# First block of a Fourier-mixing kernel: G's products in other accumulator banks, another order of a step, and identity products in TensorE's waits

## The chip, the cores and the metric

The kernel runs on one core of one Trainium2 chip. The metric is the time of the whole kernel on the device, in microseconds; the profile is one execution taken by the hardware profiler, and all positions in it are counted from the start of its span.

## What is computed

```python
X = np.fft.fft(x, axis=1)            # x: (8, 3008, 256)
X = np.fft.fft(X, axis=2)
h = X.real.reshape(8 * 3008, 256) @ w_in     # w_in: (256, 2048)
r = np.maximum(h, 0.0)
out = (r * r) @ w_out                # w_out: (2048, 256)
```

Everything is float32. The real part of the two transforms is a sum of a cosine part and a sine part. The transform along the rows (3008 long) is made by products with cosine and sine tables, after folding rows that share a table value. The transform along the 256 columns is not made on the data at all: it is multiplied into w_in, which gives a matrix G. G1 holds the cosine rows, G2 the sine rows, and gE the row of the alternating column (+1, -1, ...).

## The kernel before, in words

**The opening.** VectorE folds the rows of batch 0, tile by tile: `for_p(t)` makes the cosine half of tile t and `for_q(t)` its sine half (lines 356 to 386). TensorE multiplies the folded tiles by the tables. There are six transforms (cosine, alternating column, sine, each for two parities), each of five pieces: `even_n` (products of four tiles, L455, and a copy of the first part by ScalarE, L463), `join_4` and `join_2` (sums and differences on VectorE, L468 to L472), `odd_n` (products of three tiles of 377 columns, L455) and `join_1` (the last sums into Pt, Qt or Et, L468 to L472). Piece i of the list is `groups[i]`; `i % 5` is 0 for `even_n` and 3 for `odd_n`. The order in which pieces and folds are issued is written out by hand in the calls of `groups_at`, `for_p` and `for_q`. The tables cosT and sinT are loaded on the same DMA queue behind x.

**Weights.** w_in and w_out come as 8-byte floats, and each of 16 pieces (`load_win(j)`, `load_wout(j)`) is made float32 on the chip. Such a conversion has a beginning (two VectorE instructions, L234 and L239, and three ScalarE ones, L236, L237 and L241) and a `finish` (three VectorE instructions, L244 to L247). A piece of w_in is then multiplied by the cosine and sine tables of the columns (cosd, sind; L262), and ScalarE copies the results from PSUM into G1 and G2 (L263); four more products with the column altd give gE (L268), which ScalarE scales by 0.5 (L270). The conversions run one ahead of their use (`next_weight`).

**The blocks.** A batch is cut into blocks of up to 251 columns (CK), and a block has eight steps, j = 0 to 7 (NJ). In a step `front` makes two pairs of products with G1 and G2 (hP L551, hQ L552) in the two buffers of tag h, and VectorE makes g from each pair (L554, L556, L557). `combine` applies Relu and Square on ScalarE (L566, L567). `back` multiplies g by w_out two steps later (LAG). In the very first block, i < 8, w_out's sums are not there yet, so `back` is plain: eight products into the accumulators mA and mB (L591). From the second block on it takes seven products with sums of g (GpSimd, L574 to L577) and of w_out, into mA to mD (L604). The first block's steps also carry the conversions: after `back`, the products for the next G are issued (the list `products`), in the same PSUM buffers of tag h that `front` uses, and then the conversions of one piece (first step, last two steps) or two. Side work for the next batch is issued by `between` from the second block on.

PSUM has 2 buffers of tag h, 2 of tag d (the transforms, pe), and the four accumulators mA to mD. In the first block mC and mD are allocated but nothing is written into them.

Of the kernel before, what the change touches and what calls it, by code (L numbers as in the profile page):

```python
# [8 lines left out]
F32 = mybir.dt.float32  # L9
# [4 lines left out]
P = 128  # L14
# [67 lines left out]
def kernel(  # L82
# [12 lines left out]
    nc = tc.nc  # L95
# [65 lines left out]
    sind = const.tile([P, 2, P - 1], F32, name="sind")  # L161
    altd = const.tile([P, 2, 1], F32, name="altd")
# [6 lines left out]
    G2 = const.tile([P - 1, F], F32, name="G2")  # L169
    gE = const.tile([P, NFC], F32, name="gE")  # L170

    def load_table(tab, src, engine):
# [16 lines left out]
    for dst, src in ((cosd, cos_d), (sind, sin_d), (altd, alt_d)):  # L189
        nc.scalar.dma_start(out=dst, in_=src.rearrange("(c p) m -> p c m", p=P))  # L190


    def pair_in(j):
# [59 lines left out]
    def load_win(j):  # L253

        w = ep.tile([P, 2, CH], F32, name="win", tag="sB" if j % 2 else "sA")
        finish = convert(parts(w, 1), pair_in(j))

        def products():
            for tab, G, n in ((cosd, G1, P), (sind, G2, P - 1)):
                ps = psh.tile([P, CH], F32, name="pg", tag="h")  # L260
                for i in range(2):
                    nc.tensor.matmul(ps[0:n], tab[:, i], w[:, i], start=i == 0, stop=i == 1)  # L262
                nc.scalar.copy(G.rearrange("p (h j f) -> j p h f", h=2, j=NJ)[j],  # L263
                               ps[0:n].rearrange("p (h f) -> p h f", h=2))
            ps = psd.tile([P, CH], F32, name="pe", tag="d")
            for h in range(2):
                for i in range(2):
                    nc.tensor.matmul(ps[:, h:h + 1], w[:, i, h * P:(h + 1) * P], altd[:, i],  # L268
                                     start=i == 0, stop=i == 1)
            nc.scalar.mul(gE[:, j::NJ], ps[:, 0:2], 0.5)  # L270

        return finish, products

    def load_wout(j):

        return convert(wout[:, j].rearrange("p h c e -> p h (c e)"), pair_out(j)), lambda: None

    def sum_wout(j):

# [261 lines left out]
    def front(b, k0, n, j, between):  # L541

        pt, qt, et = PQE[b]
        ks = slice(k0, k0 + n)
        g = gp.tile([P, 2, 2, CK], F32, name="g", tag="g")
        for h in range(2):
            fc = j + NJ * h
            fs = slice(fc * P, (fc + 1) * P)
            ps = psh.tile([P, 2, CH], F32, name="ph", tag="h")
            hP, hQ = ps[:, 0, 0:n], ps[:, 1, 0:n]  # L550
            nc.tensor.matmul(hP, G1[:, fs], pt[:, ks], start=True, stop=True)  # L551
            nc.tensor.matmul(hQ, G2[:, fs], qt[:, ks], start=True, stop=True)  # L552
# [29 lines left out]
    def back(n, j, g, s, final):  # L582

        if j == 0:
            for nm in ("mA", "mB", "mC", "mD"):
# [15 lines left out]
        if final and j == NJ - 1:  # L601
            products = products[0:2] + products[4:7] + products[2:4]
        for nm, i, w, v in products:
            nc.tensor.matmul(acc[nm][:, i, 0:n], w, v[:, 0:n], start=j == 0 and i == 0, stop=j == NJ - 1,  # L604
                             skip_group_check=True)

    def gather(n, plain, final):


        mA, mB, mC, mD = (acc[nm] for nm in ("mA", "mB", "mC", "mD"))  # L610
        if plain:
            c = ep.tile([P, 2, 2, CK], F32, name="c", tag="c")
            for side, m in enumerate((mA, mB)):
                nc.scalar.copy(c[:, side, :, 0:n], m[:, :, 0:n])
            return c
        sA = ep.tile([P, 2, CK], F32, name="sA", tag="sA")
# [12 lines left out]
        gt(out=c[:, 0, 0, 0:n], in0=m1, in1=m2, op=ALU.add)  # L629
        if final:  # L630
            tt(out=c[:, 0, 1, 0:n], in0=u4, in1=mB[:, 1, 0:n], op=ALU.add)
            tt(out=c[:, 1, 1, 0:n], in0=u3, in1=mB[:, 1, 0:n], op=ALU.add)
            tt(out=c[:, 1, 0, 0:n], in0=u3, in1=mB[:, 0, 0:n], op=ALU.subtract)
            return c
        gt(out=c[:, 1, 0, 0:n], in0=u3, in1=m4, op=ALU.subtract)
        gt(out=c[:, 1, 1, 0:n], in0=u3, in1=m5, op=ALU.add)
        gt(out=c[:, 0, 1, 0:n], in0=u4, in1=m5, op=ALU.add)
        return c
# [41 lines left out]
                + groups + [(0.0, lambda: load_e(1))])  # L680


    weights = [lambda j=j: load_win(j) for j in range(2)]
    for j in range(NJ):
        weights.append(lambda j=j: load_wout(j))
        if j + 2 < NJ:
            weights.append(lambda j=j: load_win(j + 2))

    def next_weight():

        nonlocal begun
        (finish, products), begun = begun, weights.pop(0)() if weights else None
        finish()
        return products

    pieces = [fold(0, t) for t in range(NT)]
    start, *groups = [f for _, f in dft_ops(0)]

# [8 lines left out]
    def groups_at(*which):  # L707
        for i in which:
            groups[i]()

    begun = weights.pop(0)()
# [13 lines left out]
    for_q(0)  # L725
    for_q(1)
    groups_at(1, 2)
    for_p(5)
    groups_at(6, 7)
    for_p(6)  # L730
# [4 lines left out]
    groups_at(9, 10)  # L735
    for_q(6)
    groups_at(11, 12, 13)
    begun = weights.pop(0)()
    groups_at(15)
    for_q(2)  # L740
    groups_at(14, 16, 17, 18)
    for_q(3)
    groups_at(20, 19, 25)
    products = [next_weight()]
    groups_at(21, 22, 23, 26, 27, 28)
    next_weight()
    groups_at(24, 29)
    LAG = 2
    BLOCKS = [(k0, min(CK, NKT - k0)) for k0 in range(0, NKT, CK)]
    steps = [(b, k0, n, j) for b in range(B) for k0, n in BLOCKS for j in range(NJ)]  # L750
# [3 lines left out]
    def between():  # L754
# [109 lines left out]
```

## Time and profile before

| | |
|---|---|
| time, median of 3 | 1964.85 us (1961.53 to 1965.37) |
| span of the profile | 1964.0 us |
| TensorE busy | 1929.5 us, 98% |
| VectorE busy | 1399.8 us, 71% |
| ScalarE busy | 924.9 us, 47% |
| GpSimd busy | 1170.2 us, 60% |
| first front of the first block (L554) starts | 56.75 us |
| products of step 7 of the first block (L551) start | 110.22 us |

"Busy" is an average over stages with different limits: the table alone does not tell what a change in the first 110 us is worth. For this the page's slices, windows of a few microseconds and the timelines of the engines are needed. In a timeline row the first number is the start, the second the duration, and square brackets give the idle time before it and what ended it. PEclk is the clock that TensorE was granted, as a share of full speed. One float32 product shows as two records of TensorE (x2), each with a weight load (PEld).

### The profile page before, as it was taken

Reading aid. Unit: us, or ns where it says so; the run is one execution under the profiler, and the core shown is the slowest. Engines: PE = TensorE matmul, PEld = TensorE weight load, DVE = VectorE, ACT = ScalarE, POOL = GpSimd, SP = SyncE. Lnnn points to the kernel's source line nnn. Section 1 sums busy time; section 2 is a strip of 40 time slices with the busy share of each in tenths; the row PEclk is TensorE's granted clock in tenths of the full one; section 3 lists DMA queues with packets and bytes.
Section 4 is the critical chain, followed back from the end, with each engine's and each line's share of the span. In section 5 each row is a group of like instructions: output and inputs, shape, how many; then the busy total and the mean of one; then the engine's idle time right before and its main releaser. Section 6 shows DMA issues by size and latency. Waiting matters only on the chain.

```text
span 1964.0 us, 27513 instructions
## 1 busy us (share of the span) xinstructions
PE 1929.5 (98%) x9160; PEld 1708.3 (87%) x9160; DVE 1399.8 (71%) x3434; ACT 924.9 (47%) x1076; POOL 1170.2 (60%) x1705
## 2 busy tenths in 40 slices
PE   5999999999999999999999999999999999999998
PEld 4788888888988889888988889888898888988887
DVE  7889866777677776777667776677767777656554
ACT  1654544445344544444444454444544454444443
POOL 0026745667566765666557765666756676556564
PEclk7999999999999999999999999999999999999999
DMA  6332101210121111111011200121002101100101
GB/s 186 113 50 52 27 13 39 50 27 20 16 51 41 21 29 27 40 30 38 11 35 33 48 19 11 35 54 27 19 15 53 33 11 22 27 11 11 22 11 22
DMA packets 145340, 68.88 MB, mean 35 GB/s; under 512 B 129003, under 2 KB 136110, under 8 KB 145197
## 3 DMA queue, kind: packets, MB, share of 16 engines
q1 hardware_dynamic: 144121, 66.60, 15.4%
q8 instruction: 72, 1.18, 0.2%
q10 hardware_dynamic: 1076, 0.52, 0.1%
q14 instruction: 71, 0.58, 0.1%
HBM read 42.39 MB, written 24.68 MB: 34 GB/s over the span
## 4 chain that ended last, share of the span: by engine, by line
PE 93%; DVE 3%; DMA 1%; ACT 1%; issue 0%; SPq 0%; DVEq 0%; ACTq 0%
PE ph L552 16%; PE ph L551 16%; PE mC L604 16%; PE mA L604 16%; PE mB L604 16%; PE mD L604 8%; PE pd L455 3%; PE pd L500 2%; DMA xt<-in_x_dram 1%; DVE he L554 1%; DMA raw<-in_moe_w_in_dram 1%; DVE g L557 0%; DVE g L556 0%; ACT g L566 0%; ACT g L567 0%; DMA cosT<-in_cos_s_dram 0%
## 5 line engine op out<-in xcount | busy, mean ns | idle before, releaser
L566 ACT ACTIVATE g<-g 128x1004 f32<-128x1004 f32 (+1 forms) x384 | 399.5, 1040 | 818.7 <-DVE g L557 421.3
L574 POOL TENSOR_TENSOR s<-g 128x251 f32<-128x251 f32 (+1 forms) x376 | 246.1, 655 | 718.9 <-ACT g L567 657.5
L554 DVE SCALAR_TENSOR_TENSOR he<-Et,gE,ph 128x251 f32<-128x251 f32 (+1 forms) x768 | 361.8, 471 | 421.5 <-PE ph L552 420.4
L551 PE MATMUL ph<-Pt,G 128*128 128x251 f32 (+1 forms) x1536 | 451.8, 375 | 4.2 <-ACT G L263 3.4
L552 PE MATMUL ph<-Qt,G 127*128 127x251 f32 (+1 forms) x1536 | 451.4, 374 | 0.2 <-DVE Qt L468 0.2
L567 ACT ACTIVATE g<-g 128x1004 f32<-128x1004 f32 (+1 forms) x384 | 399.2, 1040 | 12.2
L604 PE MATMUL mC<-s,wsum 128*128 128x251 f32 (+1 forms) x1504 | 381.4, 374 | 0.0
L604 PE MATMUL mA<-g,wout 128*128 128x251 f32 (+1 forms) x1504 | 379.8, 374 | 0.0
L556 DVE TENSOR_TENSOR g<-he,ph 128x251 f32<-128x251 f32 (+1 forms) x768 | 320.5, 417 | 54.4 <-POOL s L574 0.5
L551 PEld LDWEIGHTS ph<-Pt,G 128*128 128x128 f32 x1536 | 287.2, 189 | 42.2 <-ACT G L263 4.0
L552 PEld LDWEIGHTS ph<-Qt,G 127*128 127x128 f32 x1536 | 291.2, 190 | 36.4 <-DVE Qt L468 0.6
L604 PEld LDWEIGHTS mC<-s,wsum 128*128 128x128 f32 x1504 | 285.5, 190 | 34.6
L557 DVE TENSOR_TENSOR g<-he,ph 128x251 f32<-128x251 f32 (+1 forms) x768 | 314.2, 409 | 0.0
L604 PEld LDWEIGHTS mA<-g,wout 128*128 128x128 f32 x1504 | 282.8, 189 | 34.7 <-issue 0.6
L575 POOL TENSOR_TENSOR s<-s,g 128x251 f32<-128x251 f32 (+1 forms) x376 | 283.3, 754 | 29.5
L576 POOL TENSOR_TENSOR s<-g 128x251 f32<-128x251 f32 (+1 forms) x376 | 295.3, 785 | 0.0
L577 POOL TENSOR_TENSOR s<-g,s 128x251 f32<-128x251 f32 (+1 forms) x376 | 255.1, 678 | 0.0
L604 PE MATMUL mB<-g,wsum 128*128 128x251 f32 (+1 forms) x752 | 220.5, 374 | 0.0
L604 PE MATMUL mD<-s,wout 128*128 128x251 f32 (+1 forms) x752 | 220.3, 374 | 0.0
L604 PE MATMUL mB<-s,wout 128*128 128x251 f32 (+1 forms) x752 | 219.9, 374 | 0.0
L604 PEld LDWEIGHTS mB<-g,wsum 128*128 128x128 f32 x752 | 142.6, 190 | 17.4
L604 PEld LDWEIGHTS mD<-s,wout 128*128 128x128 f32 x752 | 141.9, 189 | 17.7
(118 smaller groups left out, 1292.1 us busy)
## 6 DMA issues: line engine op xcount, KB each, us to landing
out_dram<-os SPq DMA_DIRECT2D x376, 56.0 KB
xt<-in_x_dram SPq DMA_DIRECT2D x32, 384.0 KB
xt<-in_x_dram SPq DMA_DIRECT2D x42, 128.0 KB
Et<-e_dram SPq DMA_DIRECT2D x7, 752.5 KB
xt<-in_x_dram SPq DMA_DIRECT2D x9, 512.0 KB
out_dram<-os SPq DMA_DIRECT2D x288, 6.8 KB
raw<-in_moe_w_in_dram SPq DMA_DIRECT2D x16, 256.0 KB
raw<-in_moe_w_out_dram SPq DMA_DIRECT2D x16, 256.0 KB
```

Of the source, the lines that this page charges most:

```text
L551: nc.tensor.matmul(hP, G1[:, fs], pt[:, ks], start=True, stop=True)
L552: nc.tensor.matmul(hQ, G2[:, fs], qt[:, ks], start=True, stop=True)
L554: nc.vector.scalar_tensor_tensor(out=t, in0=et[:, ks], scalar=gE[:, fc:fc + 1], in1=hP, op0=ALU.mult, op1=ALU.add)
L556: tt(out=g[:, h, 0, 0:n], in0=t, in1=hQ, op=ALU.add)
L557: tt(out=g[:, h, 1, 0:n][:, ::-1], in0=t, in1=hQ, op=ALU.subtract)
L566: act(v, v, AF.Relu)
L567: act(v, v, AF.Square)
L574: gt(out=s1, in0=g21, in1=g22, op=ALU.add)
L575: gt(out=s2, in0=s1, in1=g11, op=ALU.subtract)
L576: gt(out=s3, in0=g11, in1=g21, op=ALU.subtract)
L577: gt(out=s4, in0=g12, in1=s2, op=ALU.subtract)
L604: nc.tensor.matmul(acc[nm][:, i, 0:n], w, v[:, 0:n], start=j == 0 and i == 0, stop=j == NJ - 1, skip_group_check=True)
```

## The change

It does five things.

1. Identity products: `awake(n)` issues n products of the identity matrix with itself, 128 x 128, into a buffer in mB that nothing reads. 36 stand ahead of all other TensorE work, 12 behind the first products of G, and five behind each `even_n` and each `odd_n` of the opening. They are for keeping TensorE's clock up while it waits.
2. The products for G go to the accumulators mC and mD, which the first block does not use, rather than to the buffers of tag h.
3. gE comes from G2: the alternating column is the 128th column of sind, so G2 has it as row 127, and two products with the last column of the identity bring it to a column. VectorE scales it by 0.5 in place of ScalarE.
4. A step of the first block is issued in another order: behind `front` the beginning of a conversion of w_out, the products of the next G, the finish of w_in's conversion and the beginning of the one after; then Relu and Square, then `back`, then gE's products, the finish of w_out's conversion and gE's scaling. Conversions of w_in run two steps ahead.
5. In the opening, only the conversion of piece 1 of w_in is finished and that of piece 2 begun; the conversion of piece 0 of w_out, which was finished there, moves into step 1.

```diff
+    filled = psm.tile([P, CH], F32, name="filled", tag="mB")
+    def awake(n):
+        for _ in range(n):
+            nc.tensor.matmul(filled[:, 0:P], ident, ident, start=True, stop=True)
...
         def products():
-            for tab, G, n in ((cosd, G1, P), (sind, G2, P - 1)):
-                ps = psh.tile([P, CH], F32, name="pg", tag="h")
+            for tab, G, nm in ((cosd, G1, "mC"), (sind, G2, "mD")):
+                pg = psm.tile([P, CH], F32, name="pg", tag=nm)
...
+        def for_e():
             ps = psd.tile([P, CH], F32, name="pe", tag="d")
             for h in range(2):
-                for i in range(2):
-                    nc.tensor.matmul(ps[:, h:h + 1], w[:, i, h * P:(h + 1) * P], altd[:, i],
-                                     start=i == 0, stop=i == 1)
-            nc.scalar.mul(gE[:, j::NJ], ps[:, 0:2], 0.5)
+                fc = j + NJ * h
+                nc.tensor.matmul(ps[:, h:h + 1], G2[:, fc * P:(fc + 1) * P], ident[:, P - 1:], start=True, stop=True)
+            return lambda: nc.vector.tensor_scalar_mul(gE[:, j::NJ], ps[:, 0:2], 0.5)
...
     def groups_at(*which):
         for i in which:
             groups[i]()
+            if i % 5 in (0, 3):
+                awake(5)
...
     start()
+    awake(36)
     for_p(0)
-    finish, products = begun
+    finish, products, for_e = win[0]
     finish()
     products()
+    awake(12)
     for t in range(1, 4):
         for_p(t)
     groups_at(0, 5)
...
     groups_at(1, 2)
+    for_e()()
     for_p(5)
...
-    products = [next_weight()]
-    groups_at(21, 22, 23, 26, 27, 28)
-    next_weight()
-    groups_at(24, 29)
+    win.append(load_win(2))
+    win[1][0]()
+    groups_at(21, 22, 23, 26, 27, 28, 24, 29)
...
+    def weights():
+        now = i - 1 if i < NJ - 1 else i
+        late = [load_wout(now)] if now >= 0 else []
+        if i + 1 < NJ:
+            win[i + 1][1]()
+        if i + 2 < NJ:
+            win[i + 2][0]()
+        if i + 3 < NJ:
+            win.append(load_win(i + 3))
+        elif i == NJ - 2:
+            late.append(load_wout(i))
+        def rest():
+            if i + 1 < NJ:
+                late.append(win[i + 1][2]())
+            for f in late:
+                f()
+        return rest
...
             g = front(b, k0, n, j, between)
             if i < NJ:
+                rest = weights()
                 s = combine(n, g, True)
...
-        for f in products:
-            f()
-        products = [next_weight() for _ in range(2 if 0 < i < NJ - 2 else 1 if i < NJ else 0)]
+        if i < NJ:
+            rest()
```

More of the change, by code (lines that the diff above doesn't have):

```diff
@@ L160 @@
     cosd = const.tile([P, 2, P], F32, name="cosd")
-    sind = const.tile([P, 2, P - 1], F32, name="sind")
-    altd = const.tile([P, 2, 1], F32, name="altd")
+    sind = const.tile([P, 2, P], F32, name="sind")
     cosT = const.tile([P, 2, WT], F32, name="cosT")
@@ L168 @@
     G1 = const.tile([P, F], F32, name="G1")
-    G2 = const.tile([P - 1, F], F32, name="G2")
+    G2 = const.tile([P, F], F32, name="G2")
     gE = const.tile([P, NFC], F32, name="gE")
@@ L188 @@
     nc.vector.memset(ramp[:, 1:2], 255.0 * 2.0 ** 23)
-    for dst, src in ((cosd, cos_d), (sind, sin_d), (altd, alt_d)):
+    for dst, src in ((cosd, cos_d), (sind[:, :, 0:P - 1], sin_d), (sind[:, :, P - 1:], alt_d)):
         nc.scalar.dma_start(out=dst, in_=src.rearrange("(c p) m -> p c m", p=P))
+    filled = psm.tile([P, CH], F32, name="filled", tag="mB")
+    def awake(n):
+        for _ in range(n):
+            nc.tensor.matmul(filled[:, 0:P], ident, ident, start=True, stop=True)
     def pair_in(j):
@@ L258, in products @@
         def products():
-            for tab, G, n in ((cosd, G1, P), (sind, G2, P - 1)):
-                ps = psh.tile([P, CH], F32, name="pg", tag="h")
+            for tab, G, nm in ((cosd, G1, "mC"), (sind, G2, "mD")):
+                pg = psm.tile([P, CH], F32, name="pg", tag=nm)
                 for i in range(2):
-                    nc.tensor.matmul(ps[0:n], tab[:, i], w[:, i], start=i == 0, stop=i == 1)
+                    nc.tensor.matmul(pg, tab[:, i], w[:, i], start=i == 0, stop=i == 1)
                 nc.scalar.copy(G.rearrange("p (h j f) -> j p h f", h=2, j=NJ)[j],
-                               ps[0:n].rearrange("p (h f) -> p h f", h=2))
+                               pg.rearrange("p (h f) -> p h f", h=2))
+        def for_e():
             ps = psd.tile([P, CH], F32, name="pe", tag="d")
             for h in range(2):
-                for i in range(2):
-                    nc.tensor.matmul(ps[:, h:h + 1], w[:, i, h * P:(h + 1) * P], altd[:, i],
-                                     start=i == 0, stop=i == 1)
-            nc.scalar.mul(gE[:, j::NJ], ps[:, 0:2], 0.5)
-        return finish, products
+                fc = j + NJ * h
+                nc.tensor.matmul(ps[:, h:h + 1], G2[:, fc * P:(fc + 1) * P], ident[:, P - 1:], start=True, stop=True)
+            return lambda: nc.vector.tensor_scalar_mul(gE[:, j::NJ], ps[:, 0:2], 0.5)
+        return finish, products, for_e
     def load_wout(j):
-        return convert(wout[:, j].rearrange("p h c e -> p h (c e)"), pair_out(j)), lambda: None
+        return convert(wout[:, j].rearrange("p h c e -> p h (c e)"), pair_out(j))
     def sum_wout(j):
@@ L551, in front @@
             nc.tensor.matmul(hP, G1[:, fs], pt[:, ks], start=True, stop=True)
-            nc.tensor.matmul(hQ, G2[:, fs], qt[:, ks], start=True, stop=True)
+            nc.tensor.matmul(hQ, G2[0:P - 1, fs], qt[:, ks], start=True, stop=True)
             t = hp.tile([P, CK], F32, name="he", tag="he")[:, 0:n]
@@ L584, in back @@
         if j == 0:
-            for nm in ("mA", "mB", "mC", "mD"):
+            for nm in ("mA", "mB") if s is None else ("mA", "mB", "mC", "mD"):
                 acc[nm] = psm.tile([P, 2, CH], F32, name=nm, tag=nm)
@@ L607, in gather @@
     def gather(n, plain, final):
-        mA, mB, mC, mD = (acc[nm] for nm in ("mA", "mB", "mC", "mD"))
+        mA, mB = acc["mA"], acc["mB"]
         if plain:
@@ L615, in gather @@
             return c
+        mC, mD = acc["mC"], acc["mD"]
         sA = ep.tile([P, 2, CK], F32, name="sA", tag="sA")
@@ L680, in ahead @@
                 + groups + [(0.0, lambda: load_e(1))])
[L683 to L694, printed above, removed]
     pieces = [fold(0, t) for t in range(NT)]
@@ L709, in groups_at @@
             groups[i]()
-    begun = weights.pop(0)()
+            if i % 5 in (0, 3):
+                awake(5)
+    win = [load_win(0)]
     for t in range(NT):
@@ L737 @@
     groups_at(11, 12, 13)
-    begun = weights.pop(0)()
+    win.append(load_win(1))
     groups_at(15)
```

## The prediction

> **What bounds the kernel now.** I read the page first, then windows of the opening 60 us, then the timeline of each engine there, then the chain of waits through one step of the first block.
>
> The page: TensorE is busy for 98% of the span, and one slice, the first (49 us), stands out.
>
> ```profile
> PE   5999999999999999999999999999999999999998
> DVE  7889866777677776777667776677767777656554
> PEclk7999999999999999999999999999999999999999
> ```
>
> So anything the change can win or lose lies ahead of about 115 us. After it TensorE is the bound (windows of 10 us from 120 to 200 show 9.48 to 10.00 busy), and a shift of its start is carried to the end one for one. Two stretches are separate: the opening (to 55 us) and the first block's eight steps (55 to 115 us).
>
> The windows of the opening, each 3.4 us. Columns: length, PE, PEld, DVE, ACT, POOL busy, PEclk, DMA share, GB/s.
>
> ```profile
> 16.00:19.40 3.40, 0.62 (x7) 0.57 (x6) 3.26 (x9) 0.33 (x2) 0.00 (x0) 0.97 0.57 124
> ...
> 22.80:26.20 3.40, 3.16 (x9) 2.03 (x8) 3.17 (x12) 0.30 (x2) 0.00 (x0) 0.50 1.00 251
> 26.20:29.60 3.40, 2.61 (x4) 1.46 (x5) 3.26 (x10) 0.00 (x0) 0.00 (x0) 0.50 0.33 71
> 29.60:33.00 3.40, 3.40 (x7) 1.92 (x6) 2.63 (x7) 0.00 (x0) 0.00 (x0) 0.52 0.83 241
> 33.00:36.40 3.40, 3.39 (x15) 2.03 (x14) 2.96 (x9) 0.24 (x1) 0.00 (x0) 1.00 1.05 279
> 36.40:39.80 3.40, 1.49 (x9) 1.06 (x8) 2.73 (x9) 1.81 (x3) 0.00 (x0) 0.98 1.06 369
> ```
>
> Half clock from 19.4 to 33, full clock only after a window in which TensorE was busy throughout, half again after a window with 1.49 of 3.40 busy. VectorE is busy 2.6 to 3.3 of 3.4 us throughout: it is nearly the bound here too, and its gaps, from the timeline of VectorE, are only 1.40 (22.9), 0.87 (33.3), 0.60 (a DMA), 1.68 (45.0), 0.40 and 0.89 (55.4) us. Removing every one of them gives 6 us: no more than that can be won in the opening.
>
> A step of the first block, from the chain of waits (start, us, engine, tile and line):
>
> ```profile
> 73.80 1.05 ACT g L566
> ...
> 75.91 0.53 ACT G L263 x2
> ...
> 76.52 0.62 ACT fd L236
> ...
> 77.16 0.73 ACT fd L237
> ...
> 77.92 0.69 DVE fd L244
> ```
>
> The same stretch in the timelines of TensorE and VectorE, with the idle time before a row in brackets:
>
> ```profile
> 74.78 0.95 PE L268 MATMUL pe<-altd,win 128*128 128x1 f32 x8
> 76.22 0.69 PE L551 MATMUL ph<-Pt,G 128*128 128x251 f32 x2 [0.49 <-ACT G L263]
> 77.92 0.69 DVE L244 SCALAR_TENSOR_TENSOR fd<-raw,fd 128x512 uint32<-128x512 uint32 x1 [0.75 <-ACT fd L237]
> ```
>
> A step takes 8.50 us (VectorE's front starts at 71.36, 79.85, 88.35), and the chain is a loop: front, Relu and Square on ScalarE, the copies of G and the conversion's activations queued behind them, VectorE's conversion, the next front. VectorE waits 0.75 us in it, TensorE about 0.8.
>
> [...] records of 377 columns start 0.63 us apart at half clock and 0.31 at full, and the clock flips at multiples of 3.4 us. [...] the eight one-column records above take 0.95 us with some 0.17 of tail, 0.11 each[...].
>
> **The change part by part.**
>
> 1. *Price of an identity product.* It is two records of 128 columns. Warm, 251 columns take 0.21 us (products of L551 start 0.43 apart for two records), so 128 take 0.107; the load floor is 0.11. Some pairs may not overlap fully: 0.22 to 0.27 for a product, I take 0.24, so five cost 1.2. Cold: 2 x 0.213 = 0.43, five 2.1.
>
> 2. *36 + 12 ahead of the transform.* 36 run from about 1.4 us, 8 to 16 of them cold: 8 x 0.43 + 28 x 0.24 = 10.2 to 16 x 0.43 + 20 x 0.24 = 11.7, ending at 11.6 to 13.1. They lie in the 11.96 us before win's first product; a delay of up to 1 us there is hidden, as G is next read by the new gE product at about 27. The 12 end near 17. After that the cosine tables are still landing (loads of group 0 are at 19.36, 20.07, 21.59), TensorE does only some 1 us of work in 17.5 to 21.5, and by the 36.40 row the clock then drops. So I expect group 0 and 5 cold as before: the 48 gain nothing.
>
> 3. *gE's new place.* The product is queued behind group 0, five, group 5, five; its scaling (a 128x2 row, 0.1 us) is now on VectorE behind the joins of group 0 and **ahead of for_p(5)**. Behind it wait everything VectorE does, and TensorE's group 3. Group 0 ends at 22.5; 2.1 cold; group 5 cold 2.0 (22.6 to 24.7 now), 26.6; five partly warm 1.2, 27.8; hence gE at about 28.1. VectorE reaches it at 23.9 (its last join starts at 23.62): a new wait of 4.2 us (2.0 if warm: 22.1 + 1.1 + 1.0 + 1.1 + 0.6 = 25.9). Then for_p(5), the joins and for_p(6) end at 32.2 where they ended at 28.05.
>
> 4. *The fives in the opening.* From there TensorE has group 3's last product 0.63, groups 8, 13, 18, 23, 28 at 1.89 each (6 x 0.314) and 10, 15, 20, 25 at about 1.0 each: 14.1 us warm. Between them stand nine fives, 45 x 0.24 = 10.8. 32.2 + 24.9 = 57.1, if it never waits and never goes cold. It will do both about once, after its wait for VectorE at 28 to 31: a window at half clock costs 1.7 us, partly in the wait's shadow, so I add 1.5: group 28 ends at 58.6; now it ends at 55.4. Warm products save about 10 us of TensorE here, and the products that keep it warm cost 10.8: that is the whole account. The conversion of wout 0 (2.6 us of VectorE) leaves the opening, but VectorE is no longer what ends it. **Opening: +3.2 us.**
>
> 5. *The steps.* pg goes to mC and mD instead of the pair that the front reads: no wait for L557. pe: two products for four, -0.5 us. G's copies move ahead of Relu and Square: no 0.49 wait. Then TensorE needs 1.7 + 1.7 + 3.4 + 0.5 = 7.3 and VectorE 2.33 (front) + 2 x 0.67 + 2.0 + 1.95 + 0.1 = 7.75, which becomes the bound. Step 0 has one conversion: 5.0. Step 1 goes by ScalarE's order: from front 0, win 3's activations start at 4.6 and take 2.1, Relu and Square 2.1, wout 0's 2.1, G's copies 0.6; then pe 0.7, hP and hQ 0.9, hops 0.3: front 2 at 13.4, so step 1 takes 8.4. TensorE idles some 4 us in it, so that step 2 starts cold: +1.0. Steps 2 to 4: 7.75. Step 5: 7.3. From front 6 to step 7's products: 2.7 + 2.1 + 0.6 + 0.9 = 6.3. Sum 5.0 + 8.4 + 1.0 + 23.25 + 7.3 + 6.3 = 51.3; now 56.75 to 110.22 = 53.5. **Steps: -2.2 us.** This holds though one conversion more (wout 0) is in them.
>
> 6. *Nothing:* the third table into sind's last column (same three DMAs), G2's row 127, mC and mD unallocated in the first block, one activation less a step (ScalarE had room).
>
> Sum +1.0; VectorE reaches step 8 about 2 us further behind TensorE than now, for which I add 0.1. 1964.85 + 1.1 = 1966.0.
>
> **Rivals.** *The clock comes and goes (slower).* If the fives don't fill whole windows where VectorE makes TensorE wait, two windows of 30 to 37 us are cold (1.7 each) and step 2 loses 0.9 more; with 0.27 for a product (45 x 0.03 = 1.35) the opening is 57.1 - 55.4 + 3.4 + 1.35 = +6.5, the steps -1.3: +5.2, 1970.0. For: the 22.80 row stayed cold with 3.16 of 3.40 busy. Against: the fives fill just those gaps. *The clock holds (faster).* Warm from 19.4 on at 0.22 a product: gE's wait is 2.0, so TensorE's tail starts at 30.1 and takes 14.1 + 9.9 = 24.0, to 54.1: opening -1.3; steps without the cold spell -3.2; sum -4.5: 1960.4. [...] Against: the sparse work up to 21.5. *VectorE swallows it (no change):* from 130 to 160 VectorE is 9.46 to 9.52 of 10 us busy, so if it sets the pace there once it lags, TensorE's lead after the steps (-2.2) is lost and only the opening's +3.2 shows: 1968.1.
>
> **How the numbers follow.** The likeliest case, with the last rival near it, has 0.5 and spreads over -2.5 to +3.5; the slow rival 0.28, the fast one 0.22. The range 1961.0 to 1971.0 leaves out half of the fast case and the end of the slow one, 2 in 10 together. A change under 3.9 us (0.2%) counts as none: faster 0.22, same 0.5, slower 0.28.
>
> **What would show it.** Right: the scaling of gE waits 2 to 4.5 us for TensorE at 24 to 28; from 32 us TensorE has hardly an idle gap; the first front starts at about 60; steps 2 to 4 are 7.7 to 7.9 apart; the clock drops in step 1. Wrong: full clock at 22 to 27; identity products over 0.27 or under 0.22 us; steps still 8.5 apart, or under 7.5; VectorE waiting for raw loads; a changed rate after 120 us.

## The result, and the profile after

The changed kernel takes 1968.9 us (median; 1968.51 to 1970.36). The kernel before, run beside it on the same chip, takes 1963.82 us (1959.88 to 1965.37). The ratio, taken over the runs and not from the two medians, is 1.003, 95% interval 1.0018 to 1.0043: slower by about 0.3%. The forecast was 1966.0, range 1961 to 1971. The time lies in the range, but the change was forecast as 1.1 us and is 5.1 us between the medians, and the likeliest outcome of the forecast was "no change".

The two profiled executions differ less than the medians: spans of 1964.0 and 1966.7 us. The one of before was among the slower of its kernel (1965.78 us), the one of after the fastest of its kernel (1968.51 us). Both differences have to be explained.

The page of after. The first slice is fuller for TensorE and less full for VectorE, and its clock is up:

```profile
PE   8899999999999999999999999999999999999998
...
DVE  6899866777677776777667776677767777655554
...
PEclk9999999999999999999999999999999999999999
```

That is what identity products do to an average: 49 us at nearly full clock, and a later end. What follows is where the time lies.

**The opening.** Windows of after, in before's columns (length, PE, PEld, DVE, ACT, POOL busy, PEclk, DMA share, GB/s):

```profile
17.00:20.40 3.40, 0.89 (x4) 0.79 (x4) 3.23 (x10) 0.00 (x0) 0.00 (x0) 0.91 0.37 74
20.40:23.80 3.40, 3.15 (x13) 2.62 (x13) 1.60 (x7) 0.24 (x1) 0.00 (x0) 0.50 0.84 250
23.80:27.20 3.40, 3.40 (x18) 3.40 (x18) 0.26 (x2) 0.24 (x1) 0.00 (x0) 0.58 0.85 181
34.00:37.40 3.40, 3.40 (x22) 2.64 (x21) 3.33 (x10) 0.00 (x0) 0.00 (x0) 1.00 0.54 174
```

The column PEclk, read in short windows, has half clock from 19.8 to 26.6. In before it has it from 19.2 to 32.9, and in truth TensorE was slow there from its start: the four records of win's first product at 11.96 took 2.08 us, where they take 1.02 in a later step (81.43). In after they take 1.10 (11.77): of the records of the 36 identity products ahead of them, 20 lie in the 4.23 us up to 5.60 and 49 in the 5.27 us from 6.50, which is 0.42 and 0.22 us a product. So the clock comes up while they run, and it is at half again from 19.8, when TensorE has just begun the transform (19.36) after 2.95 us without work. From 26.6 the clock is full to 71.0, through the windows where before's had dropped twice more (39.7 to 46.5 and 49.9 to 53.3). But VectorE does 0.26 us of work in 23.80 to 27.20, where it had been nearly always busy. The timelines of TensorE and VectorE in after say why (start, us, engine, line and tile; in brackets the idle time before the row and its releaser):

```profile
22.48 2.34 PE L197 MATMUL filled<-ident 128*128 128x128 f32 x10
...
26.68 1.28 PE L197 MATMUL filled<-ident 128*128 128x128 f32 x10
27.79 0.50 PE L278 MATMUL pe<-ident,G 128*128 128x1 f32 x4
28.33 0.16 DVE L280 TENSOR_SCALAR gE<-pe 128x2 f32<-128x2 f32 x1 [4.28 <-PE pe L278]
...
32.51 0.90 PE L465 MATMUL pd<-cosT,w 120*128 120x377 f32 x2 [1.67 <-DVE w L396]
...
57.15 1.28 PE L197 MATMUL filled<-ident 128*128 128x128 f32 x10
59.32 0.48 DVE L564 SCALAR_TENSOR_TENSOR he<-Et,gE,ph 128x251 f32<-128x251 f32 x1 [0.96 <-PE ph L562]
```

Five identity products at half clock (2.1 us) and five at full clock (1.1 us) stand in TensorE's queue ahead of gE's two products. VectorE stands at gE's scaling for 4.28 us, with all its folds behind it. From 32.51 TensorE no longer waits, and the first front starts at 59.32 instead of 56.75: 2.57 us later.

**The steps.** By TensorE the order of a step does what it should: from the first front to step 7's products are 51.53 us, where they were 53.47. But the first front to the fifteenth takes 90.34 us (59.32 to 149.66), where it took 90.11 (56.75 to 146.86). So nothing is won. Two places stand out. The first, step 1, is contained in the 51.53 us and keeps the gain small. Timelines of ScalarE and TensorE of after:

```profile
67.98 0.71 ACT L243 ACTIVATE fd<-fd,ramp 128x512 f32<-128x512 uint32 x1
68.72 0.72 ACT L244 ACTIVATE fd<-fd,ramp 128x512 uint32<-128x512 f32 x1
69.35 0.66 ACT L248 ACTIVATE raw<-raw 128x512 f32<-128x512 uint32 x1
69.90 0.63 ACT L270 COPY G<-pg 128x256 f32<-128x256 f32 x2
...
70.58 0.66 PE L278 MATMUL pe<-ident,G 128*128 128x1 f32 x4 [4.12 <-ACT G L270]
```

The products of G were done at about 66.4 (the last begin at 65.65), but the copies stand on ScalarE behind Relu and Square and behind the three activations of w_out's conversion. TensorE waits 4.12 us, and its clock is at half from 71.0 to 74.4. The forecast had both, with "some 4 us".

The second place, the end of the stretch, takes back what was won. VectorE and TensorE of after, steps 6 and later:

```profile
109.12 0.69 DVE L251 SCALAR_TENSOR_TENSOR fd<-raw,fd 128x512 uint32<-128x512 uint32 x1 [0.54 <-ACT fd L244]
...
110.85 0.67 PE L561 MATMUL ph<-Pt,G 128*128 128x251 f32 x2
...
111.59 0.69 DVE L251 SCALAR_TENSOR_TENSOR fd<-raw,fd 128x512 uint32<-128x512 uint32 x1 [0.45 <-ACT fd L244]
...
113.80 0.47 DVE L564 SCALAR_TENSOR_TENSOR he<-Et,gE,ph 128x251 f32<-128x251 f32 x1
...
118.09 0.69 DVE L251 SCALAR_TENSOR_TENSOR fd<-raw,fd 128x512 uint32<-128x512 uint32 x1 [1.21 <-ACT fd L244]
...
123.10 0.69 PE L561 MATMUL ph<-Pt,G 128*128 128x251 f32 x2 [0.64 <-DVE g L567]
...
143.40 0.69 PE L561 MATMUL ph<-Pt,G 128*128 128x251 f32 x2 [0.89 <-DVE g L567]
```

The fronts of the same stretch in VectorE's timeline of before:

```profile
111.44 0.48 DVE L554 SCALAR_TENSOR_TENSOR he<-Et,gE,ph 128x251 f32<-128x251 f32 x1 [1.08 <-PE ph L552]
...
116.47 0.48 DVE L554 SCALAR_TENSOR_TENSOR he<-Et,gE,ph 128x251 f32<-128x251 f32 x1 [0.69 <-PE ph L552]
...
121.58 0.47 DVE L554 SCALAR_TENSOR_TENSOR he<-Et,gE,ph 128x251 f32<-128x251 f32 x1 [0.31 <-PE ph L552]
...
126.69 0.48 DVE L554 SCALAR_TENSOR_TENSOR he<-Et,gE,ph 128x251 f32<-128x251 f32 x1 [1.15 <-PE ph L552]
```

In before VectorE came first and waited for TensorE: its slack (the time it has to spare) was 1.08, 0.69, 0.31 and 1.15 us at fronts 7 to 10, 3.23 in all. At front 11 (132.12) there is no wait: from there VectorE has no slack in before either. In after, step 6 holds two conversions of w_out and step 7 one, each with a wait for ScalarE (0.54, 0.45 and 1.21 us), and step 6 takes 8.98 us. Front 7 starts 2.36 us later than in before (113.80 against 111.44), though TensorE made its products only 0.63 us later (110.85 against 110.22). Now VectorE has no wait at fronts 7 to 11, and TensorE waits for the front's buffers. How much later after is than before, step by step:

| position | later than before, us |
|---|---|
| first front | 2.57 |
| products of step 7 (TensorE) | 0.63 |
| products of step 9 | 0.80 |
| products of step 10 | 1.81 |
| front 11 to front 14 | 2.8 |
| end of the span | 2.7 |

From front 6, which was 0.53 us earlier than in before, to front 11, VectorE had 6.6 us more to do or to wait for than in before (30.10 us, against 26.77 with 3.23 of waits in them); 3.23 of that fell into the slack. From front 11 on the fronts keep their distance, and from 143.4 on TensorE has it too.

### The profile page after: what moved, and what is told of

It reads as the page before. It is cut to its first block, busy times and chain, and to the rows that moved or that the text cites. A ratio compares the mean times of both kernels' runs of the same rounds, so it can differ in the third digit from the quotient of the medians.

```text
span 1966.7 us, 27897 instructions
## 1 busy us (share of the span) xinstructions
PE 1943.3 (99%) x9344; PEld 1727.8 (88%) x9344; DVE 1402.9 (71%) x3442; ACT 924.5 (47%) x1068; POOL 1169.1 (59%) x1705
## 4 chain that ended last, share of the span: by engine, by line
PE 93%; DVE 4%; DMA 1%; ACT 1%; issue 0%; SPq 0%; DVEq 0%; ACTq 0%
PE ph L561 16%; PE ph L562 16%; PE mC L614 16%; PE mA L614 16%; PE mB L614 16%; PE mD L614 8%; PE pd L465 3%; PE pd L510 2%; PE filled L197 1%; DVE he L564 1%; DMA xt<-in_x_dram 1%; DVE g L566 1%; DVE g L567 1%; DVE m L253 0%; DVE fd L251 0%
```

## The experiments

Times are medians, each compared with the kernel before run in the same sitting (its medians: 1963.7 to 1964.1). The opening is counted from the first copy of group 0 (tile da, by ScalarE) to the first front, because that copy starts anywhere between 21.1 and 23.3 us from one execution to the next; the transform's products ahead of it wait for the tables (2.77 us for cosT in before, 2.95 in after). The steps are the first front to the fifteenth. The last two columns come from one profiled execution each.

| kernel | time, us | ratio to before (95%) | opening | steps |
|---|---|---|---|---|
| before, trace above | | | 34.12 | 90.11 |
| before_again (one run) | 1963.41 | | 31.78 | 90.10 |
| after | 1968.9 | 1.003 (1.0018 to 1.0043) | 36.59 | 90.34 |
| no_identity | 1965.78 | 1.0007 (0.9998 to 1.0016) | 32.50 | 90.85 |
| no_fives | 1966.19 | 1.0009 (1.0001 to 1.0018) | 32.74 | 90.91 |
| ge_late | 1966.89 | 1.0012 (1.0003 to 1.0021) | 34.46 | 91.50 |
| identity_alone | 1965.13 | 1.0002 (0.9993 to 1.001) | 33.83 | 90.09 |
| wout0_opening | 1968.67 | 1.0027 (1.0016 to 1.0038) | 36.82 | 90.44 |
| steps_alone | 1966.86 | 1.0012 (1.0005 to 1.0019) | 34.79 | 91.06 |
| steps_wout0 | 1964.94 | 1.0008 (0.9999 to 1.0017) | 34.15 | 89.44 |
| g_first | 1967.28 | 1.0019 (1.0011 to 1.0027) | 37.29 | 88.73 |
| banks_alone | 1964.1 | 1.0 (0.9992 to 1.0009) | 31.32 | 90.26 |
| steps_wout0_g_first | 1961.92 | 0.999 (0.9981 to 0.9999) | 34.15 | 87.04 |

### The kernel before once more: how much the opening moves by itself

The same code, to see whether the changes of the clock fall elsewhere.

> The kernel before, unchanged, for a second trace of its opening. Theory (its spread of several us comes from where the clock's windows fall and when the tables land): another set of half-clock stretches, with the first front moved by 0.5 us or more against the first trace and the steps from the first front on within 0.3 us of it. Rival (the spread comes from elsewhere): the same opening, and a difference after 60 us.

The windows of this execution:

```profile
22.80:26.20 3.40, 3.40 (x11) 2.71 (x10) 3.10 (x11) 0.36 (x2) 0.00 (x0) 0.50 0.97 272
26.20:29.60 3.40, 2.27 (x7) 1.05 (x6) 3.26 (x10) 0.00 (x0) 0.00 (x0) 0.97 0.41 91
```

In the execution of the prediction the same window was 3.16 of 3.40 busy and the clock stayed at half until 32.9. Here it was 3.40, and the clock rose at its end, at 26.4. The first front starts at 54.47 instead of 56.75 while the steps differ by 0.01 us, and the spans differ by 2.4 us. VectorE waits for TensorE's products for 4.3 us in the opening of the one and for 1.5 in that of the other, so the difference comes in at TensorE, at half clock to 32.9 in the one and to 26.4 in the other; that the place of the clock's changes alone made it, two executions can't show. So the profile that I forecast from had an opening on the slow side, and one and the same code moves by 2.3 us there. The openings without identity products in the table lie between 31.3 and 34.8, but part of that is their code.

### Identity products: all away, the fives away, or alone

```diff
# no_identity, from after
-        for _ in range(n):
+        for _ in range(0):
# no_fives, from after (the 36 and the 12 stay)
-            if i % 5 in (0, 3):
-                awake(5)
# identity_alone, from before: filled and awake as in after, and
+            if i % 5 in (0, 3):
+                awake(5)
...
     start()
+    awake(36)
...
     products()
+    awake(12)
```

> The changed kernel without any identity product (all 36, 12 and 60 left out; nothing of the output depends on them). Theory (the fives delay gE's scaling, which VectorE waits for, and then fill TensorE; their price eats the clock's gain): gE's scaling waits only about 1.6 us instead of 4.3, the opening is at half clock again, the first front starts at about 58 (59.3 with them), the steps are unchanged, so 1 us faster than the changed kernel, about 1968. Rival (the identity products earn their place, the loss is elsewhere): the opening at half clock costs 3 us or more beyond the changed kernel's, first front at 62 or later, 1972.

> The changed kernel with the 36 and the 12, without the fives. Theory (the 48 gain nothing, since TensorE is cold again before the tables have landed): within 0.7 us of the kernel without any identity product, about 1968. Rival (the 48 keep the clock up for groups 0 and 5): full clock from 19 to 26 us, gE's wait under 1 us, 2 us faster than without any, 1966.

> The kernel before with the identity products alone (36, 12 and five behind each even_n and odd_n; gE and the steps as before). Theory (without gE's wait the clock's gain of about 10 us of TensorE and the products' 10.8 nearly cancel, and the opening is a little shorter): first front at 54.5 to 56.5, the whole 0.5 to 2.5 us faster than the kernel before. Rival (the products stand in the way): 2 us or more slower than the kernel before.

Without any of them the changed kernel takes 1965.78 us, about 3 us less where 1 was expected, and its interval (to 1.0016) lies below that of after (from 1.0018). Its first front, expected at about 58, starts at 54.42. The wait for gE, in VectorE's timeline of no_identity:

```profile
24.68 0.16 DVE L280 TENSOR_SCALAR gE<-pe 128x2 f32<-128x2 f32 x1 [1.42 <-PE pe L278]
```

1.42 us instead of 4.28, 2.86 less: in after the ten identity products in front of it take 2.14 and 1.11 us. With the 36 and the 12 kept (no_fives) opening (32.74 against 32.50) and time (+0.4, intervals nearly the same) stay: the 48 bring the clock up early (win's four records at 12.35 take 1.03 us, in no_identity 2.07 at 11.48), and when gE's four records come, at 24.72, these take 0.85 us, as in no_identity, where in after at full clock they take 0.50: it is at half again. They gain nothing, as forecast.

Given to the kernel before (identity_alone), the products do neither of the things expected of them: not 0.5 to 2.5 us faster, and not 2 us slower. The time is the same (0.9993 to 1.001), the steps are unchanged to 0.02 us, and the opening is within those of before. Its windows:

```profile
22.80:26.20 3.40, 3.40 (x17) 3.40 (x16) 2.49 (x8) 0.24 (x1) 0.00 (x0) 0.50 1.02 318
...
36.40:39.80 3.40, 3.40 (x22) 2.63 (x21) 3.27 (x11) 1.59 (x4) 0.00 (x0) 1.00 0.90 298
39.80:43.20 3.40, 3.40 (x28) 3.24 (x27) 2.56 (x9) 0.91 (x3) 0.00 (x0) 1.00 0.41 143
```

The row 36.40, where before did 1.49 us of work and lost its clock, is now busy throughout, and the clock holds. Yet TensorE is full: what it saves at full clock it spends on identity products. So the products alone cost nothing and give nothing; in after they cost, because gE's scaling waits behind ten of them. The other half of that comparison is below: with the scaling moved away, the kernel takes the same time with the products (ge_late, 1966.89 us) and without them (steps_alone, 1966.86).

### gE's scaling where nothing waits for it

The products go behind group 17 and the scaling behind `for_q(3)`.

```diff
-    for_e()()
     for_p(5)
...
-    groups_at(14, 16, 17, 18)
+    groups_at(14, 16, 17)
+    scale_e = for_e()
+    groups_at(18)
     for_q(3)
+    scale_e()
```

> The changed kernel with gE's products and scaling moved from behind the first joins to behind the joins of the fourth transform, where VectorE does not wait for them. Theory (the 4.3 us wait is what makes the opening longer): for_p(6) ends near 28 instead of 32.5, the first front starts at 55.2 to 56, the whole is 3.5 to 4 us faster than the changed kernel, about 1965. Rival (TensorE, filled with fives, bounds the opening anyway and the wait lies in its shadow): first front at 58 or later, at most 1 us faster, 1968.

The median falls by 2.0 us, to 1966.89, and the opening by 2.1 (its interval overlaps that of after at 1.0018 to 1.0021). The wait is gone, but 3.5 to 4 us were expected. VectorE and TensorE of ge_late show the rest:

```profile
26.54 0.25 DVE L478 TENSOR_TENSOR db<-da,pd 128x94 f32<-128x94 f32 x1 [1.58 <-ACT da L473]
...
29.05 0.90 PE L465 MATMUL pd<-cosT,w 120*128 120x377 f32 x2 [0.23 <-DVE w L396]
...
56.49 0.48 DVE L564 SCALAR_TENSOR_TENSOR he<-Et,gE,ph 128x251 f32<-128x251 f32 x1 [0.96 <-PE ph L562]
```

Of the 4.28 us, 1.58 come back at once: the joins of group 5 wait, because its products stand behind five identity products too. TensorE's unbroken stretch then begins 7.0 us behind the first copy of group 0 (29.05), where in after it begins 9.8 behind it (32.51). In both kernels TensorE is full from there to the first front, some 26 us, with gE's products in it in ge_late, and in both VectorE waits for it at the end by the same amounts (1.64, 2.01 and 0.96 us, in after 1.64, 2.00 and 0.96). So the opening gains 2.1.

### The new order of the steps alone

After without identity products and with gE late: the opening is then like that of before, apart from the conversions.

> The changed kernel without any identity product and with gE's scaling moved behind the joins of the fourth transform: the steps' new order and banks alone. Theory (the steps won nothing in all, since the late steps give it back; the opening loses gE's wait of 1.4 us and the conversion of piece 0 of w_out): opening, from the first copy of group 0 to the first front, 31 to 32 us (34.1 in the kernel before), the steps 90.3 to 91; 2 us faster than the kernel before. Rival (the new order by itself is slower): slower than the kernel before.

It was expected to be 2 us faster than before, and is 0.12% slower (1.0005 to 1.0019). The order of the steps, the part meant to gain, is no gain. The waits of TensorE in its timeline:

```profile
68.37 1.01 PE L278 MATMUL pe<-ident,G 128*128 128x1 f32 x4 [4.12 <-ACT G L270]
...
121.62 0.69 PE L561 MATMUL ph<-Pt,G 128*128 128x251 f32 x2 [0.64 <-DVE g L567]
...
141.92 0.69 PE L561 MATMUL ph<-Pt,G 128*128 128x251 f32 x2 [0.89 <-DVE g L567]
```

The same three as in after, to 0.01 us. They belong to the order of the steps and not to the identity products.

The opening is not the gain that was expected of it either (34.79 us, where 31 to 32 were). VectorE of steps_alone:

```profile
36.83 0.43 DVE L241 TENSOR_SCALAR fd<-raw 128x512 uint32<-128x512 uint32 x1 [1.47 <-DMA raw<-in_moe_w_in_dram]
```

VectorE, which no longer waits 1.42 us for gE as in no_identity, comes to the next piece of w_in before it has landed and waits 1.47 us for it. In no_identity there is no such wait; before has it with 0.60 us and before_again with 1.47. In the three kernels here without identity products and with the late scaling it is 0.81 to 1.47 us. So of the 1.42 us that gE's wait took at most 0.6 are won by its removal.

### The conversion of w_out's piece 0 back in the opening

```diff
-    win.append(load_win(2))
+    wout_0 = load_wout(0)
     win[1][0]()
-    groups_at(21, 22, 23, 26, 27, 28, 24, 29)
+    groups_at(21, 22, 23, 26, 27, 28)
+    win.append(load_win(2))
+    wout_0()
+    groups_at(24, 29)
...
-        now = i - 1 if i < NJ - 1 else i
-        late = [load_wout(now)] if now >= 0 else []
+        late = [load_wout(i + 1)] if i + 1 < NJ else []
...
-        elif i == NJ - 2:
-            late.append(load_wout(i))
```

wout0_opening is after with this edit, steps_wout0 is steps_alone with it. Each step converts a piece of w_out one earlier, so steps 6 and 7 have one conversion less each.

> The changed kernel with the conversion of piece 0 of w_out back in the opening, so that step i converts piece i+1 and steps 6 and 7 have one and none instead of two and one. Theory (the lag of VectorE at steps 7 to 10, from one conversion more in the block and two of them in step 6, gives back what the steps won): from the first front to the fifteenth 87.5 to 88.5 us instead of 90.3, the opening at most 1 us longer since VectorE idles 3.6 us at its end; 1.5 to 2.5 us faster than the changed kernel. Rival (what is given back comes from ScalarE's order or from the cold clock of step 2): 90 us as before, no faster.

> The same with the conversion of piece 0 of w_out in the opening as well. Theory (two causes add up): opening 32 to 33 us, first to fifteenth front 87.5 to 88.5, 3 to 4 us faster than the kernel before. Rival (the block's VectorE work was hidden): no faster than the steps alone.

VectorE's lag at the end is gone. TensorE of wout0_opening has no wait from 110 to 150 us; VectorE waits for it again. TensorE in step 0, and VectorE at front 8:

```profile
64.41 1.01 PE L278 MATMUL pe<-ident,G 128*128 128x1 f32 x4 [2.86 <-ACT G L270]
...
119.03 0.47 DVE L564 SCALAR_TENSOR_TENSOR he<-Et,gE,ph 128x251 f32<-128x251 f32 x1 [2.69 <-PE ph L562]
```

But step 0 now has w_out's conversion, and takes 8.33 us instead of 5.19; TensorE waits 2.86 us in it and 1.51 in step 1. The steps stay at 90.44 where 87.5 to 88.5 was expected, and the time at 1968.67. In steps_wout0 they fall to 89.44, but 3 to 4 us less than before were expected, and it takes 1964.94 us (0.9999 to 1.0017): no gain. So the conversion can be paid for at the front or at the end. That paying it early helps only if it doesn't hold up G's copies is what the last run below speaks for.

### G's products ahead of w_out's conversion

Within a step G's products are issued ahead of the beginning of w_out's conversion, so that on ScalarE G's copies come ahead of its three activations.

```diff
-        late = [load_wout(now)] if now >= 0 else []
         if i + 1 < NJ:
             win[i + 1][1]()
+        late = [load_wout(now)] if now >= 0 else []
```

> The changed kernel with one order turned: a step's products for the next G, and ScalarE's copies of them, are issued ahead of the beginning of w_out's conversion instead of behind it. Theory (TensorE's 4.1 us wait in step 1, and the half clock of step 2 behind it, come from G's copies queued behind that conversion's activations on ScalarE): the wait falls to 2 us or less, step 2 is at full clock (7.9 instead of 8.3), TensorE's products of step 7 start 51 us or less after the first front (51.5), but what lies behind step 8 is VectorE's and stays: 0.5 to 1.5 us faster than the changed kernel. Rival (VectorE alone sets the steps): no difference.

ScalarE and TensorE of g_first in step 1:

```profile
68.15 0.63 ACT L270 COPY G<-pg 128x256 f32<-128x256 f32 x2
68.67 0.73 ACT L243 ACTIVATE fd<-fd,ramp 128x512 f32<-128x512 uint32 x1
...
68.83 0.61 PE L278 MATMUL pe<-ident,G 128*128 128x1 f32 x4 [2.20 <-ACT G L270]
```

The wait falls from 4.12 to 2.20 us, by the activations that are no longer ahead. And the clock holds. Windows of g_first, and then the corresponding ones of after:

```profile
67.40:70.80 3.40, 1.97 (x11) 1.83 (x12) 3.33 (x8) 3.37 (x7) 0.00 (x0) 1.00 0.10 22
70.80:74.20 3.40, 3.40 (x18) 3.00 (x17) 3.21 (x8) 3.33 (x5) 0.00 (x0) 1.00 0.82 252
```

```profile
68.00:71.40 3.40, 0.82 (x5) 0.82 (x6) 3.33 (x7) 3.33 (x8) 0.00 (x0) 0.94 0.33 103
71.40:74.80 3.40, 3.40 (x10) 2.77 (x10) 2.20 (x7) 3.05 (x4) 0.00 (x0) 0.56 0.65 205
```

Step 1 takes 7.93 us instead of 8.65, and step 7's products start 48.3 us after the first front instead of 51.5. Of these 3.2 us only 1.6 arrive at the fifteenth front (88.73 against 90.34), since VectorE's lag is still there: TensorE waits 0.55, 0.64 and 0.89 us for the front's buffers. That the clock holds is not the order's doing alone: in steps_wout0_g_first below, which has it too, the front's pairs of records at 67.38, 68.36 and 69.19 take 1.04 to 1.19 us, where those of the next step take 0.59 to 0.67 (from 76.11). The median is 1.6 us below after's; the intervals overlap.

### The banks alone

```diff
# from before
-            for tab, G, n in ((cosd, G1, P), (sind, G2, P - 1)):
-                ps = psh.tile([P, CH], F32, name="pg", tag="h")
+            for tab, G, n, nm in ((cosd, G1, P, "mC"), (sind, G2, P - 1, "mD")):
+                ps = psm.tile([P, CH], F32, name="pg", tag=nm)
```

mC and mD are not allocated in the first block, as in after.

> The kernel before with G's products in mC and mD and nothing else changed. Theory (the step's loop goes through Relu, Square, G's copies and the conversion's activations on ScalarE, so a buffer wait of TensorE beside it is hidden): TensorE's waits for L557 ahead of the products for G vanish, the steps stay 8.5 us apart, within 0.7 us of the kernel before. Rival (the shared buffers held the steps back): steps of 8.2 us, 2 us faster.

No difference (0.9992 to 1.0009), and steps of 8.50 us as before. TensorE no longer waits for the pair of buffers ahead of G's products, but a little longer behind them:

```profile
72.47 0.69 PE L551 MATMUL ph<-Pt,G 128*128 128x251 f32 x2 [0.62 <-ACT G L263]
```

0.62 us for ScalarE's copies, where before had 0.49. The wait for the buffers was not on the loop that sets the step.

### All repairs together

steps_wout0 with G's products first: no identity products, gE late, w_out's piece 0 in the opening.

> No identity products, gE's scaling behind the joins of the fourth transform, w_out's piece 0 in the opening, and G's products issued ahead of w_out's conversion: what the earlier runs speak for, together. Theory: opening like the kernel before (32 to 34 us from the first copy of group 0 to the first front, by the clock's luck), first to fifteenth front 88.5 to 89.4 instead of 90.1; 0.5 to 1.5 us faster than the kernel before. Rival (the block is as long in any order): no faster than the kernel before.

1961.92 us, ratio 0.999 (0.9981 to 0.9999): 0.1% faster than before, by an interval that ends just short of 1, and 7.0 us below after. The steps take 87.04 us, 3.1 less than before and 1.5 less than the best that was expected. TensorE of this kernel:

```profile
66.71 0.81 PE L278 MATMUL pe<-ident,G 128*128 128x1 f32 x4 [2.99 <-ACT G L270]
...
93.45 1.10 PE L269 MATMUL pg<-win,cosd 128*128 128x256 f32 x4 [0.42 <-DVE win L254]
```

Fronts 0 to 5 are 7.92 to 7.94 us apart, in step 1 too, in spite of TensorE's wait of 2.99 us and the slow front behind it (1.04 to 1.19 us a pair): there TensorE has time to spare. The waits for the front's buffers of 0.64 and 0.89 us are gone; the first one left (0.75 us at 157.26) stands in before too (0.76 at 160.52). In the steady steps TensorE waits 0.42 us for VectorE's conversion: VectorE is the bound of a step, as the forecast had it.

## Why the prediction was right or wrong

**Identity product, 0.22 to 0.27, 0.24 taken: right.** Ten records take 1.11 us, 0.222 a product, and five cold ones 2.14 us against 2.1.

**The 48 gain nothing: right.** 36 run from 1.37 to 11.77 ahead of win's products (at 0.42 us each up to about 6 us, so some 11 of them cold, where 8 to 16 was an estimate), groups 0 and 5 are at half clock from 19.8, and no_fives against no_identity shows no gain.

**gE's new wait, 4.2: right.** It is 4.28, and `for_p(6)`'s product starts at 32.51 against 32.2. Its removal was worth 2.1 us in the opening, not the whole, as 1.58 come back at group 5's joins and TensorE is full behind them.

**The fives, and +3.2 for the opening: right in kind, near in size by two errors of opposite sign.** TensorE is full from 32.5, group 28's products end at about 57.2, as the sum without a cold window has it (57.1), and the opening is +2.57 between the traces. The extra 1.5 for a cold window, an estimate, was not needed: the clock holds from 26.6 to 71.0. But the five products behind group 28, 1.1 us ahead of the first front's (57.15 to 58.27), are not among the nine fives of the sum. That what the clock gives the products take back is what identity_alone shows. In the reading of the opening, VectorE is not busy 2.6 to 3.3 us in every window: those from 19.40, 43.20 and 53.40 have 2.00, 1.72 and 2.07, with the gaps that the forecast lists.

**The steps to step 7's products, -2.2: right in size.** -1.94 was measured. Step 0 took 5.19 (5.0), step 1 8.65 (8.4), steps 2 to 4 8.31, 8.30 and 7.92 (7.75 and 1.0 once). gE's scaling takes 0.27 us of VectorE's time in a step (81.20 to 81.47), where 0.1 was reckoned. That VectorE is the bound of a step was right; that TensorE is the bound of all that comes after 115 us was not, as the next step shows.

**The failed step: "VectorE reaches step 8 about 2 us further behind TensorE than now, for which I add 0.1."** The lag was too small and its price far too small. Front 7 is 2.36 us later than in before and TensorE's products for it 0.63, a lag of 1.7; at front 8 it is 3.56 and 0.61, a lag of 2.95. From step 7's products to the fronts from 11 on the distance to before grows from 0.63 to 2.8 us, about 2.2, where 0.1 was added. The trace of before shows how little room there was: 3.23 us of slack at fronts 7 to 10 and none at front 11, and VectorE, with a third conversion of w_out and 2.20 us of waits for ScalarE in steps 6 and 7, used up more than that. wout0_opening and steps_wout0, which have one conversion less there, have no wait of TensorE for the front's buffers up to 150 us. With 2.2 for this term the three terms are 2.57 - 1.94 + 2.2 = 2.8, which is what the traces differ by, against the 1.1 forecast.

The other part of the miss is no step of the sum. The profile that I worked from was 0.9 us above the median that I added to, and after's profile 0.4 below its median. That makes 1.3 us of 2.9. before_again shows where such differences lie: the opening of before is 2.3 us shorter in another execution, while the three profiled openings with the fives and the wait for gE lie within 36.6 to 37.3 us. The median that I added to was also 1.0 us above the one measured beside after (1963.82), so that the time lies nearer to the forecast than the change does; that much of the agreement is luck.

**The rivals.** "VectorE swallows it" (1968.1) is what happened: the steps' gain is lost and the opening's shows. It was filed as a spread of the likeliest case and should have been that case. "The clock comes and goes" did not: no cold window between 26.6 and 71.0. "The clock holds" failed at its start, since the clock fell at 19.8; what it would have been worth no run shows, but from 34 us TensorE was full at full clock too.

Of the signs named beforehand as proof against the forecast, identity products outside 0.22 to 0.27 did not appear. A changed rate after 120 us did: 2 of the 2.8 us arise between step 9's products (121.33) and TensorE's wait at 143.40, and only from there on is the rate that of before. The steps 2 and 3 are at 8.3, between "7.7 to 7.9" and "still 8.5". With G's products first, steps 1 and 2 of g_first are at 7.93; its step 3 is 8.30 again, in steps_wout0_g_first it is 7.93. In g_first and in after VectorE idles 0.49 and 0.48 us ahead of the front that ends step 3 (88.84 and 89.77); why is open.

That steps_alone, which has no wait for gE, is not faster than no_identity, which has one of 1.42 us (1.0005 to 1.0019 against 0.9998 to 1.0016), is in part the wait for w_in's piece that takes its place (1.47 us). The rest of the distance between their openings (34.79 and 32.50) lies in waits for TensorE, and is as large as that between the two executions of before.

## What to carry to other kernels

Before a gain on one engine is counted, look in the trace for the next places where another engine waits for it, up to the first where it doesn't wait, and read off how long: the sum of these waits (3.23 us here, in one trace of before) is about the extra work or waiting that the other engine can take without charge. What is beyond it has to be priced, with the new waits that the extra work brings (2.20 us for ScalarE here). Products that only keep the clock up are paid in the queue of the engine that they keep up (here 0.22 us each at full clock, 0.43 at half). No run here gained by them; where TensorE had no time to spare they took back what the clock gave, and they must not stand ahead of a small result that a busy engine needs. Removing a wait is worth its length only if nothing stands close behind it: of 4.28 us the opening gained 2.1, and of 1.42 us at most 0.6. When work is reordered in a step, follow each engine's queue: G's copies behind another conversion's activations on ScalarE made TensorE wait 4.12 us, and ahead of them 2.20.

## What the runs showed of the hardware that was not expected

In the first 100 us PEclk changes in before at 19.2, 32.9, 39.7, 46.5, 49.9 and 53.3 us, and in after at 19.8, 26.6, 71.0 and 74.4: within each of the two traces 3.41 us or a multiple of it apart. The forecast's "full clock only after a window in which TensorE was busy throughout" fits both: in the 3.41 us ahead of each of the five rises TensorE has 3.41 or 3.42 us of busy time, and in before, after 3.32 us of it in the 3.41 us from 22.64, the clock stays at half. It does not fit before_again:

```profile
39.80:43.20 3.40, 2.69 (x5) 1.53 (x6) 3.09 (x10) 0.02 (x1) 0.00 (x0) 0.54 0.05 20
43.20:46.60 3.40, 3.36 (x19) 2.52 (x17) 2.43 (x6) 0.24 (x1) 0.00 (x0) 0.96 0.00 0
```

There nearly all of the second row is at full clock, behind a row with 2.69 us busy. Nor did the clock fall only behind idle stretches: in the 3.41 us ahead of its falls at 39.7 and 49.9 in before TensorE was busy for 1.60 and 1.69 us. What decides is open.

The column PEclk shows nothing of the time ahead of its first change: in before it reads 1.00 from 11.96 to 14.00, where win's four records took 2.08 us against 1.02 later, half speed.

Six runs of before are spread over 5.5 us, six of after over 1.9. That the identity products make the time steadier is not shown by that: the runs of identity_alone, which has the same products, are spread over 4.4 us, and over 2.9 in their spans.
